# Linear attention and gated layers on one core: the attention denominators of four chunks in one PSUM tile, their reciprocals spread over the rows by DMA

## The chip, the cores and the metric

The kernel runs on one core of a Trainium2 chip. Its time is the device time of one execution in microseconds (us). TensorE (PE) multiplies, VectorE (DVE) and ScalarE (ACT) read its sums from PSUM and work on them, GpSimd (POOL) only fills constants, SyncE (SP) issues nearly all transfers.

## The reference

The input x has 2048 rows of 1024 numbers in bf16. Four layers follow each other: attention, gated, attention, gated. Each normalises its rows first and adds its result to x.

```python
# attention: 32 heads of 32
pq, pk = phi(q), phi(k)              # phi(t) = where(t > 0, t + 1, exp(t)) + 1e-6
kv  = einsum("bhsd,bhse->bhde", pk, v)
z   = einsum("bhsd->bhd", pk)        # per head: sum of pk over all rows
num = einsum("bhqd,bhde->bhqe", pq, kv)
den = einsum("bhqd,bhd->bhq", pq, z)[..., None] + 1e-6
x   = x + concat_heads(num / den) @ wo
# gated layer, F = 3584
x   = x + ((norm(x) @ w_gate) * (norm(x) @ w_up)) @ w_down
```

The change concerns `den`: one number for each head and row, by which the 32 elements of that head in `pq` are divided (the division is done on `pq`, ahead of the product with `kv`).

## The kernel before

Rows are taken in four groups g of 512. An attention layer has two parts. The first makes keys and values for all rows (`kv_chunk`, matmul at L230) and sums `pk` times `v` in three PSUM tiles (`kp`, L248), with a column of ones beside `v` that gives z. The second is a loop of steps i over the queries; nothing in it is reordered by a scheduler, each engine runs its instructions in the order in which the loop writes them.

In step i, `q_step` makes chunk c of group g (i = 8g + c): 128 of the 1024 query columns (four heads) for 512 rows, eight matmuls of 512 columns (L333). `phi` (L216 to L218) is an Exp on ACT and two operations on DVE; the last one frees the PSUM bank. Four steps later `den_step` multiplies the chunk by `zb[:, c, :]` (L341). `zb` is 128 by 128: z times a mask that is one inside each head's 32 by 32 block, so each denominator comes out in all 32 rows of its head. ACT makes the reciprocal as exp(-ln(d + 1e-6)) (L343, L344), and DVE writes `pq` times it into a tile `pqs` (L347). Twelve steps behind the query, `out_step` multiplies 128 rows of the scaled queries by M, eight matmuls (L354), and DVE adds the sum to X (L356).

M is `kv` times `wo`, folded once a layer: `finish_kv` masks the sums and writes `zb` (L298 to L302), `tr_kv` transposes at step 3, and `fold` (L318, two matmuls; one copy on ACT, L320, one on DVE, L322) runs at steps 4 to 11.

PSUM: query and output sums share a ring of four banks (`mm`), the sums of `kp`, denominators and folds a ring of three (`kv`). SBUF: weights, transposed inputs and M share a ring of 13 slots of 1 MB (`wp`); SP issues loads in program order and waits in that order for the slot of each. In the query loop it loads the first weights of the gated layer behind (wg, wu at L74; wd at L81): a pair at step 0, a pair and wd at step 14, wd at 17, 25, and three at 33; and it transposes the first normalised rows of the next layer (L171, steps 22 to 28). A ring `h` of four tiles of seven blocks (128 by 512) holds `pk`, `pqs` and the gated layer's products `hT`.

In the gated layer each of 28 steps f makes gate and up sums (L423, L427), ACT copies the gate (L430) into a tile `gs`, DVE multiplies (L433), and the down product follows (L459, L462).

Of the kernel before, what the change touches and what calls it, by code (L numbers as in the profile page):

```python
# [9 lines left out]
ALU = mybir.AluOpType  # L10
BF16 = mybir.dt.bfloat16
# [4 lines left out]
def kernel(  # L16
# [11 lines left out]
    nc = tc.nc  # L28
# [10 lines left out]
    FB = F // NB  # L39
    FPB = NB // P  # L40
    DC = D // NB
    HC = 7

    ctx.enter_context(tc.manual_schedule())

# [1 line left out]
    small = ctx.enter_context(tc.tile_pool(name="small", bufs=4))  # L47
    xnp = ctx.enter_context(tc.tile_pool(name="xnp", bufs=2))
    wp = ctx.enter_context(tc.tile_pool(name="wp", bufs=13))
    hp = ctx.enter_context(tc.tile_pool(name="hp", bufs=4))  # L50
    work = ctx.enter_context(tc.tile_pool(name="work", bufs=2))
    psum = ctx.enter_context(tc.tile_pool(name="psum", bufs=4, space=bass.MemoryType.PSUM))

    x_view = A_x[0].rearrange("(t p) d -> p t d", p=P)
# [62 lines left out]
    nc.gpsimd.memset(mask[:], 0.0)  # L117
    for b in range(4):
        nc.gpsimd.memset(mask[32 * b:32 * b + 32, 32 * b:32 * b + 32], 1.0)
    eps5 = const.tile([P, 1], F32, tag="eps5", name="eps5")  # L120
    nc.gpsimd.memset(eps5[:], 1e-5)
    eps6 = const.tile([P, 1], F32, tag="eps6", name="eps6")
# [91 lines left out]
    def phi(ps, dst):  # L214
        m = work.tile([P, NB], F32, tag="m", name="m", bufs=3)
        nc.scalar.activation(out=m[:], in_=ps[:], func=ACT.Exp)  # L216
        nc.vector.tensor_scalar(out=m[:], in0=m[:], scalar1=1.0, scalar2=1e-6, op0=ALU.min, op1=ALU.add)  # L217
        nc.vector.scalar_tensor_tensor(out=dst, in0=ps[:], scalar=0.0, in1=m[:], op0=ALU.max, op1=ALU.add)  # L218

    def layer_A(li, preload_B):  # L220
# [67 lines left out]

        kvm = work.tile([P, KD, P], BF16, tag="kvm", name="kvm", bufs=1)
        kvT = work.tile([P, KD, P], BF16, tag="kvT", name="kvT", bufs=1)  # L290
        zb = work.tile([P, KD, P], BF16, tag="zb", name="zb", bufs=1)
        z = work.tile([P, KD], F32, tag="z", name="z", bufs=1)

        def finish_kv():
            for b in range(3):
                nb = min(3, KD - 3 * b)
                src = kvp[b][:, 0:nb * VW].rearrange("p (c f) -> p c f", f=VW)
                nc.vector.tensor_copy(out=z[:, 3 * b:3 * b + nb], in_=src[:, :, P])  # L298
                for j in range(nb):
                    nc.vector.tensor_tensor(out=kvm[:, 3 * b + j, :], in0=src[:, j, 0:P], in1=mask[:], op=ALU.mult)  # L300
            for c in range(KD):
                nc.vector.tensor_scalar(out=zb[:, c, :], in0=mask[:], scalar1=z[:, c:c + 1], scalar2=None,  # L302
                                        op0=ALU.mult)

        def tr_kv():
# [15 lines left out]
                else:  # L321
                    nc.vector.tensor_copy(out=M[n][:, c, :], in_=ps[:])  # L322

        pq = {}
        pqs = {}

        def q_step(g, c):
            xnT = xnTs[(li, g)]
            w = wA["q"][c // (NB // P)]
            j = c % (NB // P)  # L330
            ps = mm_tile()
            for k in range(KD):
                nc.tensor.matmul(out=ps[:], lhsT=w[:, k, j * P:(j + 1) * P], rhs=xnT[:, k, :],  # L333
                                 start=(k == 0), stop=(k == KD - 1))
            pq[(g, c)] = work.tile([P, G], BF16, tag="pq", name="pq", bufs=6)
            phi(ps, pq[(g, c)][:])

        def den_step(g, c):
            p = pq.pop((g, c))
            dps = kv_tile("dps")  # L340
            nc.tensor.matmul(out=dps[:], lhsT=zb[:, c, :], rhs=p[:], start=True, stop=True)  # L341
            r = work.tile([P, G], F32, tag="r", name="r", bufs=2)
            nc.scalar.activation(out=r[:], in_=dps[:], func=ACT.Ln, bias=eps6[:], scale=1.0)  # L343
            nc.scalar.activation(out=r[:], in_=r[:], func=ACT.Exp, scale=-1.0)  # L344
            if c % 4 == 0:
                pqs[(g, c // 4)] = hp.tile([P, HC, G], BF16, tag="h", name="pqs")
            nc.vector.tensor_tensor(out=pqs[(g, c // 4)][:, c % 4, :], in0=p[:], in1=r[:], op=ALU.mult)  # L347

        def out_step(g, j):
            tl, n = divmod(j, DC)  # L350
            t = g * TPG + tl
            ps = mm_tile("ops")
            for c in range(KD):
                nc.tensor.matmul(out=ps[:], lhsT=pqs[(g, c // 4)][:, c % 4, tl * P:(tl + 1) * P],  # L354
                                 rhs=M[n][:, c, :], start=(c == 0), stop=(c == KD - 1))
            nc.vector.tensor_tensor(out=X[:, t, n * NB:(n + 1) * NB], in0=X[:, t, n * NB:(n + 1) * NB],  # L356
                                    in1=ps[:], op=ALU.add)

        LAG, OLAG = 4, 12
        NQ = NG * KD  # L360
        for i in range(NQ + OLAG):
            if i >= LAG and i - LAG < NQ:
                den_step(*divmod(i - LAG, KD))
            if i < NQ:
                q_step(*divmod(i, KD))
            if i == 0:
                for t in range(NT - TPG, NT):
                    kp(t)
                finish_kv()
                preload_B("p")  # L370
            if i == 3:
                tr_kv()
            if 4 <= i < 4 + KD:
                fold(i - 4)
            if i >= OLAG:
                out_step(*divmod(i - OLAG, KD))
            if i in (14, 17, 25, 33):
                preload_B({14: "pr", 17: "r", 25: "r", 33: "rrr"}[i])
            for u in range(TPG):
# [31 lines left out]
    def layer_B(li, stream):  # L411
        last = li == 3
        for g in range(NG):
            xnT = xnTs[(li, g)]
            hT = []
            nl, ng = (li, g + 1) if g + 1 < NG else (li + 1, 0)
            for f in range(KF):
                fb, j = divmod(f, FPB)
                if j == 0:
                    wg, wu = stream.have.pop((g, fb))  # L420
                gp = mm_tile("gp")
                for k in range(KD):
                    nc.tensor.matmul(out=gp[:], lhsT=wg[:, k, j * P:(j + 1) * P], rhs=xnT[:, k, :],  # L423
                                     start=(k == 0), stop=(k == KD - 1))
                up = mm_tile("up")
                for k in range(KD):
                    nc.tensor.matmul(out=up[:], lhsT=wu[:, k, j * P:(j + 1) * P], rhs=xnT[:, k, :],  # L427
                                     start=(k == 0), stop=(k == KD - 1))
                gs = work.tile([P, NB], F32, tag="gs", name="gs", bufs=2)
                nc.scalar.copy(out=gs[:], in_=gp[:])  # L430
                if f % HC == 0:
                    hT.append(hp.tile([P, HC, G], BF16, tag="h", name="hT"))
                nc.vector.tensor_tensor(out=hT[f // HC][:, f % HC, :], in0=gs[:], in1=up[:], op=ALU.mult)  # L433
                if j == FPB - 1:
                    stream.pair()
                    stream.rows()
                for u in range(TPG if nl < 4 else 0):
                    t = ng * TPG + u
                    if f == 6 + 4 * u:
                        ln_stats(nl, (t,))  # L440
                    if f == 7 + 4 * u:
                        ln_norm(nl, t)
                    if f == 8 + 4 * u:
                        tr_tile(nl, t)
            xnTs.pop((li, g))
            if g == NG - 1 and not last:
                wA["k"] = load_A(1)
                wA["v"] = load_A(2)
                wA["q"] = load_A(0)
                wA["o"] = load_wo()  # L450
            for tl in range(TPG):
                t = g * TPG + tl
                cuts = [(n * NB, (n + 1) * NB) for n in range(DC)]
                if last and t == NT - 1:
                    cuts[-1:] = [(D - NB, D - NB // 2), (D - NB // 2, D)]
                for lo, hi in cuts:
                    ps = kv_tile("dn", hi - lo)
                    for f in range(KF):
                        nc.tensor.matmul(out=ps[:], lhsT=hT[f // HC][:, f % HC, tl * P:(tl + 1) * P],  # L459
                                         rhs=stream.wd[f // 4][:, f % 4, lo:hi],  # L460
                                         start=(f == 0), stop=(f == KF - 1))
                    nc.vector.tensor_tensor(out=X[:, t, lo:hi], in0=X[:, t, lo:hi], in1=ps[:], op=ALU.add)  # L462
                    if last:
                        nc.sync.dma_start(out=o_view[:, t, lo:hi], in_=X[:, t, lo:hi])
# [47 lines left out]
```

## Time and profile before

| | |
|---|---|
| median of the runs | 1654.07 us (1654.0 to 1654.95, three runs) |
| the profiled execution's own time | 1654.75 us |
| its span, first to last instruction | 1652.9 us |
| granted TensorE clock | 1.00 |
| denominator matmuls (L341) | 64, each 379 ns long in the records |
| Ln and Exp of the reciprocals (L343, L344) | 64 each, 692 and 629 ns |
| scaling of the queries on DVE (L347) | 64, 685 ns |
| copies of M (L320 ACT, L322 DVE) | 16 each, 579 and 680 ns |
| query loop of the first attention layer | about 126 to 250 us |
| load of 1 MB, issue to landing (wg, wd) | 5.2 and 5.6 us, median |

A matmul's record is longer than the time for which it holds the array, since the next one starts before its end: the spacing of the starts tells its cost. In the rows of single instructions the first number is the start, the second the length, both in us from the start of the span; `L341` is a line of the kernel, `dps<-pq,zb` what is written from what. "Idle before" is what the engine waited for.

### The profile page before, as it was taken

What the parts mean: (1) busy time and instruction counts of PE and PEld (TensorE: products, weight loads), DVE (VectorE), ACT (ScalarE), POOL (GpSimd) and SP (SyncE); (2) the same over time, 40 slices, a digit from 0 to 9 for tenths busy, and PEclk for the clock granted to TensorE, in tenths of its full rate; (3) what the DMA queues carried; (4) which work ended last, traced back from release to release, by engine and by line L of the source; (5) the groups of instructions that cost most, each with busy time, mean ns of one, the idle gap of its engine ahead of it and who ended that gap; (6) DMA issues with size and microseconds to landing.
All of it is one profiled execution on the core that took longest, in us unless ns stands there. A gap on an engine that the chain in (4) does not pass through costs nothing.

```text
span 1652.9 us, 18521 instructions
## 1 busy us (share of the span) xinstructions
PE 1646.7 (100%) x7864; PEld 757.7 (46%) x7864; DVE 559.3 (34%) x985; ACT 368.0 (22%) x699; POOL 1.6 (0%) x17
## 2 busy tenths in 40 slices
PE   9999999999999999999999999999999999999999
PEld 4544444444444444444444544444444444444444
DVE  6537762311321231132155388522113212211111
ACT  4336541200210120021033375311002101100110
POOL 0000000000000000000000000000000000000000
PEclk9999999999999999999999999999999999999999
DMA  7433134631461263055132321346225514622400
GB/s 229 127 77 102 38 90 134 172 127 39 139 163 41 83 172 128 31 141 167 46 100 39 87 79 45 124 134 172 76 87 147 162 33 131 173 82 90 153 29 23
DMA packets 211250, 174.21 MB, mean 105 GB/s; under 512 B 66528, under 2 KB 202080, under 8 KB 211168
## 3 DMA queue, kind: packets, MB, share of 16 engines
q1 hardware_dynamic: 210880, 172.64, 36.2%
q8 instruction: 61, 1.00, 0.2%
q10 hardware_dynamic: 288, 0.39, 0.1%
q14 instruction: 21, 0.17, 0.0%
HBM read 153.09 MB, written 4.19 MB: 95 GB/s over the span
## 4 chain that ended last, share of the span: by engine, by line
PE 99%; DMA 0%; SPq 0%; ACT 0%; issue 0%; DVE 0%
PE dn L459 23%; PE up L427 23%; PE gp L423 23%; PE ps L230 13%; PE ops L354 7%; PE ps L333 7%; PE kvp L248 1%; PE dps L341 1%; PE mps L318 0%; DMA wv<-in_A_wqkv_dram 0%; SPq L97 0%; PE pt L180 0%; PE pt L308 0%; ACT xnT L182 0%; SPq L65 0%
## 5 line engine op out<-in xcount | busy, mean ns | idle before, releaser
L423 PE MATMUL gp<-xnT,wg 128*128 128x512 bf16 x1792 | 423.3, 379 | 0.0
L427 PE MATMUL up<-xnT,wu 128*128 128x512 bf16 x1792 | 423.3, 379 | 0.0
L459 PE MATMUL dn<-wd,hT 128*128 128x512 bf16 (+1 forms) x1820 | 388.1, 376 | 0.0
L433 DVE TENSOR_TENSOR hT<-gs,up 128x512 bf16<-128x512 f32 x224 | 154.0, 688 | 567.0 <-PE up L427 567.0
L430 ACT COPY gs<-gp 128x512 f32<-128x512 f32 x224 | 131.4, 586 | 945.8 <-PE gp L423 945.8
L459 PEld LDWEIGHTS <-hT 128*128 128x128 bf16 x1820 | 178.1, 98 | 209.0
L423 PEld LDWEIGHTS <-wg 128*128 128x128 bf16 x1792 | 175.4, 98 | 211.4
L427 PEld LDWEIGHTS <-wu 128*128 128x128 bf16 x1792 | 175.3, 98 | 211.4
L462 DVE TENSOR_TENSOR X<-X,dn 128x512 bf16<-128x512 bf16 (+1 forms) x65 | 44.1, 679 | 341.9 <-PE dn L459 341.9
L230 PEld LDWEIGHTS <-xnT 128*128 128x128 bf16 x1024 | 99.7, 98 | 120.2 <-ACT xnT L182 1.1
L333 PE MATMUL ps<-xnT,wq 128*128 128x512 bf16 x512 | 120.3, 379 | 0.0
L354 PE MATMUL ops<-M,pqs 128*128 128x512 bf16 x512 | 118.3, 379 | 0.0
L230 PE MATMUL ps<-wv,xnT 128*128 128x512 bf16 x512 | 112.8, 379 | 1.4 <-DMA wv<-in_A_wqkv_dram 0.8
L230 PE MATMUL ps<-wk,xnT 128*128 128x512 bf16 x512 | 112.6, 379 | 0.0
L216 ACT ACTIVATE m<-ps 128x512 f32<-128x512 f32 x128 | 76.4, 597 | 158.3 <-PE ps L230 130.4
L217 DVE TENSOR_SCALAR m<-m 128x512 f32<-128x512 f32 x128 | 54.1, 422 | 82.6 <-ACT m L216 81.8
L354 PEld LDWEIGHTS <-pqs 128*128 128x128 bf16 x512 | 50.1, 98 | 60.4
L333 PEld LDWEIGHTS <-wq 128*128 128x128 bf16 x512 | 50.0, 98 | 60.1 <-issue 0.6
L146 DVE BATCH_NORM_STATS2 st<-X 128x6 f32<-128x512 bf16 x120 | 76.7, 681 | 0.0
L343 ACT ACTIVATE r<-dps,eps 128x512 f32<-128x512 f32 x64 | 44.3, 692 | 54.1 <-PE dps L341 54.1
L347 DVE TENSOR_TENSOR pqs<-pq,r 128x512 bf16<-128x512 bf16 x64 | 43.8, 685 | 31.4 <-ACT r L344 31.4
L241 ACT CAST vb<-ps 128x512 bf16<-128x512 f32 x64 | 37.6, 588 | 62.1 <-PE ps L230 62.1
(45 smaller groups left out, 384.3 us busy)
## 6 DMA issues: line engine op xcount, KB each, us to landing
wg<-in_B_w_gate_dram SPq DMA_DIRECT2D x56, 1024.0 KB, 5.2
wu<-in_B_w_up_dram SPq DMA_DIRECT2D x56, 1024.0 KB, 6.9
wd<-in_B_w_down_dram SPq DMA_DIRECT2D x14, 1024.0 KB, 5.6
wk<-in_A_wqkv_dram SPq DMA_DIRECT2D x4, 1024.0 KB, 7.7
wq<-in_A_wqkv_dram SPq DMA_DIRECT2D x4, 1024.0 KB, 7.3
wo<-in_A_wo_dram SPq DMA_DIRECT2D x4, 1024.0 KB, 7.6
out_dram<-X SPq DMA_DIRECT2D x31, 128.0 KB, 1.7
X<-in_A_x_dram SPq DMA_DIRECT2D x14, 256.0 KB, 8.5
```

What stands on the lines that cost most here:

```text
L146: nc.vector.bn_stats(out=st[:, c, :], in_=X[:, t, c * FMAX:(c + 1) * FMAX])
L216: nc.scalar.activation(out=m[:], in_=ps[:], func=ACT.Exp)
L217: nc.vector.tensor_scalar(out=m[:], in0=m[:], scalar1=1.0, scalar2=1e-6, op0=ALU.min, op1=ALU.add)
L230: nc.tensor.matmul(out=ps[:], lhsT=xnT[:, k, tl * P:(tl + 1) * P], rhs=w[:, k, :], start=(k == 0), stop=(k == KD - 1))
L333: nc.tensor.matmul(out=ps[:], lhsT=w[:, k, j * P:(j + 1) * P], rhs=xnT[:, k, :], start=(k == 0), stop=(k == KD - 1))
L343: nc.scalar.activation(out=r[:], in_=dps[:], func=ACT.Ln, bias=eps6[:], scale=1.0)
L354: nc.tensor.matmul(out=ps[:], lhsT=pqs[(g, c // 4)][:, c % 4, tl * P:(tl + 1) * P], rhs=M[n][:, c, :], start=(c == 0), stop=(c == KD - 1))
L423: nc.tensor.matmul(out=gp[:], lhsT=wg[:, k, j * P:(j + 1) * P], rhs=xnT[:, k, :], start=(k == 0), stop=(k == KD - 1))
L427: nc.tensor.matmul(out=up[:], lhsT=wu[:, k, j * P:(j + 1) * P], rhs=xnT[:, k, :], start=(k == 0), stop=(k == KD - 1))
L430: nc.scalar.copy(out=gs[:], in_=gp[:])
L433: nc.vector.tensor_tensor(out=hT[f // HC][:, f % HC, :], in0=gs[:], in1=up[:], op=ALU.mult)
L459: nc.tensor.matmul(out=ps[:], lhsT=hT[f // HC][:, f % HC, tl * P:(tl + 1) * P], rhs=stream.wd[f // 4][:, f % 4, lo:hi], start=(f == 0), st ...
```

## The change

`den_step` is split. Steps, by the new line numbers:

- `q_step` writes phi straight into a tile of the ring `h`, which is now seven tiles of four chunks (`HC = 4`), in place of a tile of its own. The gated layer's `hT` uses tiles of four as well.
- `zb` is 128 by 32, by a mask `hmask` that has one eight columns wide strip for each head. `den_quad(u)` (steps 5, 9, ... 33) multiplies chunks 4u to 4u+3, each into 32 rows of one PSUM tile, with the matmul placed in a column quarter of the array (L353). One Ln and one Exp (L356, L357) then serve four chunks, and a DMA issued by ACT (L359) writes the 16 different rows, 32 KB, to a buffer in DRAM.
- `spread(u)`, behind the query of the same step, has ACT issue four transfers (L366). Each reads the four chunks' rows of one head, 8 KB, and writes them to 32 rows of `rb`: 256 KB each, 1 MB for a quad. `rb` has one buffer.
- `scale` (L372) multiplies the queries in place by `rb`, chunks 0 and 1 of a quad at step 4u+8, chunks 2 and 3 at step 4u+9.
- Output steps (L379, L381) run 16 steps behind the query instead of 12, and the eight folds (L324; copies L326 on ACT and L328 on DVE) stand at steps 4, 6, 7, 8, 10, 11, 12 and 14.
- `gs` takes its buffers from the ring `m` of three, which phi uses.

```diff
-    HC = 7
+    HC = 4
+    HW = 32
...
-    hp = ctx.enter_context(tc.tile_pool(name="hp", bufs=4))
+    hp = ctx.enter_context(tc.tile_pool(name="hp", bufs=7))
...
+    dramp = ctx.enter_context(tc.tile_pool(name="dramp", bufs=4, space=bass.MemoryType.DRAM))
...
+    hmask = const.tile([P, HW], F32, tag="hmask", name="hmask")
+    nc.gpsimd.memset(hmask[:], 0.0)
+    for b in range(4):
+        nc.gpsimd.memset(hmask[32 * b:32 * b + 32, 8 * b:8 * b + 8], 1.0)
...
-        zb = work.tile([P, KD, P], BF16, tag="zb", name="zb", bufs=1)
+        zb = work.tile([P, KD, HW], BF16, tag="zb", name="zb", bufs=1)
...
-            pq[(g, c)] = work.tile([P, G], BF16, tag="pq", name="pq", bufs=6)
-            phi(ps, pq[(g, c)][:])
-
-        def den_step(g, c):
-            p = pq.pop((g, c))
+            phi(ps, pq_at(i))
+
+        def den_quad(u):
             dps = kv_tile("dps")
-            nc.tensor.matmul(out=dps[:], lhsT=zb[:, c, :], rhs=p[:], start=True, stop=True)
-            r = work.tile([P, G], F32, tag="r", name="r", bufs=2)
+            for j in range(4):
+                i = 4 * u + j
+                nc.tensor.matmul(out=dps[HW * j:HW * j + HW, :], lhsT=zb[:, i % KD, :], rhs=pq_at(i),
+                                 start=True, stop=True, tile_position=(0, HW * j))
+            r = work.tile([P, G], F32, tag="r", name="r", bufs=1)
             nc.scalar.activation(out=r[:], in_=dps[:], func=ACT.Ln, bias=eps6[:], scale=1.0)
             nc.scalar.activation(out=r[:], in_=r[:], func=ACT.Exp, scale=-1.0)
-            if c % 4 == 0:
-                pqs[(g, c // 4)] = hp.tile([P, HC, G], BF16, tag="h", name="pqs")
-            nc.vector.tensor_tensor(out=pqs[(g, c // 4)][:, c % 4, :], in0=p[:], in1=r[:], op=ALU.mult)
+            rd = dramp.tile([4, 4, G], F32, tag="rd", name="rd")
+            nc.scalar.dma_start(out=rd[:].rearrange("h j n -> j h n"), in_=r[0:P:8, :])
+            rbs[u] = rd
+
+        def spread(u):
+            rd = rbs[u]
+            rb = work.tile([P, 4, G], F32, tag="rb", name="rb", bufs=1)
+            for h in range(4):
+                nc.scalar.dma_start(out=rb[HW * h:HW * h + HW, :, :].rearrange("p j n -> p (j n)"),
+                                    in_=rd[h, :, :].rearrange("j n -> (j n)").partition_broadcast(HW))
+            rbs[u] = rb
+
+        def scale(i):
+            nc.vector.tensor_tensor(out=pq_at(i), in0=pq_at(i), in1=rbs[i // 4][:, i % 4, :], op=ALU.mult)
...
-        LAG, OLAG = 4, 12
+        OLAG = 16
+        FOLD = [4, 6, 7, 8, 10, 11, 12, 14]
         NQ = NG * KD
         for i in range(NQ + OLAG):
-            if i >= LAG and i - LAG < NQ:
-                den_step(*divmod(i - LAG, KD))
+            if i % 4 == 1 and 8 <= i < NQ + 8:
+                for j in (2, 3):
+                    scale(i - 9 + j)
+            if i % 4 == 1 and 5 <= i < NQ + 5:
+                den_quad(i // 4 - 1)
             if i < NQ:
-                q_step(*divmod(i, KD))
+                q_step(i)
+            if i % 4 == 1 and 5 <= i < NQ + 5:
+                spread(i // 4 - 1)
+            if i % 4 == 0 and 8 <= i < NQ + 8:
+                for j in (0, 1):
+                    scale(i - 8 + j)
...
-            if 4 <= i < 4 + KD:
-                fold(i - 4)
+            if i in FOLD:
+                fold(FOLD.index(i))
...
-                gs = work.tile([P, NB], F32, tag="gs", name="gs", bufs=2)
+                gs = work.tile([P, NB], F32, tag="m", name="gs", bufs=3)
```

More of the change, by code (lines that the diff above doesn't have):

```diff
@@ L301, in finish_kv @@
             for c in range(KD):
-                nc.vector.tensor_scalar(out=zb[:, c, :], in0=mask[:], scalar1=z[:, c:c + 1], scalar2=None,
+                nc.vector.tensor_scalar(out=zb[:, c, :], in0=hmask[:], scalar1=z[:, c:c + 1], scalar2=None,
                                         op0=ALU.mult)
@@ L322, in fold, with pq_at, q_step @@
                     nc.vector.tensor_copy(out=M[n][:, c, :], in_=ps[:])
-        pq = {}
         pqs = {}
-        def q_step(g, c):
+        rbs = {}
+        def pq_at(i):
+            if i // HC not in pqs:
+                pqs[i // HC] = hp.tile([P, HC, G], BF16, tag="h", name="pq")
+            return pqs[i // HC][:, i % HC, :]
+        def q_step(i):
+            g, c = divmod(i, KD)
             xnT = xnTs[(li, g)]
@@ L334, in q_step @@
                                  start=(k == 0), stop=(k == KD - 1))
-            pq[(g, c)] = work.tile([P, G], BF16, tag="pq", name="pq", bufs=6)
-            phi(ps, pq[(g, c)][:])
-        def den_step(g, c):
-            p = pq.pop((g, c))
+            phi(ps, pq_at(i))
+        def den_quad(u):
             dps = kv_tile("dps")
-            nc.tensor.matmul(out=dps[:], lhsT=zb[:, c, :], rhs=p[:], start=True, stop=True)
-            r = work.tile([P, G], F32, tag="r", name="r", bufs=2)
+            for j in range(4):
[3 more added lines that the diff above has]
+            r = work.tile([P, G], F32, tag="r", name="r", bufs=1)
             nc.scalar.activation(out=r[:], in_=dps[:], func=ACT.Ln, bias=eps6[:], scale=1.0)
             nc.scalar.activation(out=r[:], in_=r[:], func=ACT.Exp, scale=-1.0)
-            if c % 4 == 0:
-                pqs[(g, c // 4)] = hp.tile([P, HC, G], BF16, tag="h", name="pqs")
-            nc.vector.tensor_tensor(out=pqs[(g, c // 4)][:, c % 4, :], in0=p[:], in1=r[:], op=ALU.mult)
+            rd = dramp.tile([4, 4, G], F32, tag="rd", name="rd")
[8 more added lines that the diff above has]
+            rbs[u] = rb
+            rbs[u] = rb
+        def scale(i):
+            nc.vector.tensor_tensor(out=pq_at(i), in0=pq_at(i), in1=rbs[i // 4][:, i % 4, :], op=ALU.mult)
         def out_step(g, j):
@@ L353, in out_step @@
             for c in range(KD):
-                nc.tensor.matmul(out=ps[:], lhsT=pqs[(g, c // 4)][:, c % 4, tl * P:(tl + 1) * P],
+                nc.tensor.matmul(out=ps[:], lhsT=pq_at(g * KD + c)[:, tl * P:(tl + 1) * P],
                                  rhs=M[n][:, c, :], start=(c == 0), stop=(c == KD - 1))
```

## The prediction

> **What bounds the kernel now.** I read the busy shares first, then the chain that ended last, then the stretches around the step that changes, then single instructions there.
>
> The page's busy shares and the chain by engine and line:
>
> ```profile
> PE 1646.7 (100%) x7864; PEld 757.7 (46%) x7864; DVE 559.3 (34%) x985; ACT 368.0 (22%) x699; POOL 1.6 (0%) x17
> ...
> PE 99%; DMA 0%; SPq 0%; ACT 0%; issue 0%; DVE 0%
> PE dn L459 23%; PE up L427 23%; PE gp L423 23%; PE ps L230 13%; PE ops L354 7%; PE ps L333 7%; PE kvp L248 1%; PE dps L341 1%; PE mps L318 0%; DMA wv<-in_A_wqkv_dram 0%; SPq L97 0%; PE pt L180 0%; PE pt L308 0%; ACT xnT L182 0%; SPq L65 0%
> ```
>
> TensorE is the chain, from end to end. The denominators (dps, L341) are 1% of it, so what this change can take away is small, and what it can add as a wait is paid in full. The stretches of the first attention layer (its start, its query steps without output steps, two mixed ones, its output steps alone); the columns are PE, weight loads, DVE and ACT busy, clock, DMA share and GB/s:
>
> ```profile
> 126.00:142.00 16.00, 15.97 (x104) 8.41 (x103) 11.44 (x34) 8.95 (x16) 0.00 (x0) 1.00 0.21 67
> 142.00:157.00 15.00, 15.00 (x71) 6.83 (x70) 14.79 (x27) 14.36 (x26) 0.00 (x0) 1.00 0.27 84
> 157.00:195.00 38.00, 38.00 (x178) 17.22 (x177) 27.32 (x47) 20.03 (x33) 0.00 (x0) 1.00 0.16 56
> 195.00:234.00 39.00, 39.00 (x183) 17.67 (x182) 30.59 (x55) 22.34 (x39) 0.00 (x0) 1.00 0.45 127
> 234.00:250.00 16.00, 16.00 (x76) 7.24 (x75) 7.29 (x12) 1.32 (x2) 0.00 (x0) 1.00 0.06 17
> ```
>
> The second line matters: where queries run without output steps, DVE is busy 14.79 of 15.00 us. The average of 34% hides that; a wait put into DVE's queue there can't be caught up. One step of that stretch, instruction by instruction (start, length):
>
> ```profile
> 147.65 0.38 PE L341 MATMUL dps<-pq,zb 128*128 128x512 bf16 x1
> 147.65 1.61 PEld L333 LDWEIGHTS <-wq 128*128 128x128 bf16 x8
> 147.86 1.89 PE L333 MATMUL ps<-xnT,wq 128*128 128x512 bf16 x8
> ...
> 148.37 0.70 ACT L343 ACTIVATE r<-dps,eps 128x512 f32<-128x512 f32 x1
> ...
> 149.11 0.63 ACT L344 ACTIVATE r<-r 128x512 f32<-128x512 f32 x1
> 149.11 0.68 DVE L322 CAST M<-mps 128x512 bf16<-128x512 f32 x1
> 149.37 0.31 PEld L318 LDWEIGHTS <-kvT 128*128 128x128 bf16 x2
> 149.59 0.59 PE L318 MATMUL mps<-wo,kvT 128*128 128x512 bf16 x2
> 149.77 0.69 DVE L347 TENSOR_TENSOR pqs<-pq,r 128x512 bf16<-128x512 bf16 x1
> ...
> 150.02 0.38 PE L341 MATMUL dps<-pq,zb 128*128 128x512 bf16 x1
> ```
>
> From one denominator matmul to the next are 2.37 us: eight query matmuls 1.73, two fold matmuls 0.43, the denominator 0.21. So a 512-column matmul holds the array for 0.216 us, though its record is 0.379 long; the 0.163 between them is pipeline that the next one overlaps.
>
> **Part by part.**
>
> *Removed from TensorE:* 64 denominator matmuls (32 a layer) of 0.216: 13.8 us, all on the chain.
>
> *Added to TensorE:* 16 quads of four 32-column matmuls. No row shows one. Least: all four stream at once, 0.216, so 3.5 us in all and 10.3 saved. Most: one after another, 0.864, with an emptied pipeline on entering and leaving (0.163 each) and a bare weight load (0.098): 1.29 each, 20.6, so 6.8 lost. I take one stream plus the two emptied pipelines and one load, 0.216+0.326+0.098 = 0.64: 16 of them are 10.2, **saving 3.6 us**. The reason for the middle: four column quarters hold separate weights, so nothing in the work forbids streaming together, but the matmuls before and after use the whole width. The Trainium skill, TensorEngine Tiling (Array Packing), Key Properties, states both halves: tiles operate independently, and a change of tiling mode drains the array. TensorE: Matmul & The Clock Gate, Part 3, gives 2.38x for three column tiles; with free switching the quads would be an estimated 3.5 to 4.5 us in all and the sum about 1655. No row here shows a switch.
>
> *ACT:* loses 48 Ln and 48 Exp (0.692 and 0.629: 63 us), gains 80 DMA issues. The two issues on its queue at the start last 0.39 and 0.45, so 31 to 36 us. In busy time a gain, but ACT isn't the bound; what counts is a new wait. Each spread (L366) stands in ACT's queue behind the query's Exp and waits until the 32 KB of reciprocals (L359) lie in DRAM. Let T be PE's arrival at quad u (step 4u+5). Sums are readable at T+0.6, Ln and Exp take 1.37 (148.37 to 149.74), the store is issued at T+1.95; the nearest small stores, of X to the output, land after 1.6 us, so T+3.55. Four issues hold ACT until T+5.2. The Exp of query 4u+6, ready at T+4.25, is queued behind it, then the fold's copy of M, which frees a bank of the ring of three for the next fold, and then DVE's half of phi. So 0.95 us of delay per quad. DVE's work in four such steps, by starts, is 4x(0.46+0.60) phi + 4x0.60 scale + 3x0.60 M = 8.4; PE's is 4x1.73+3x0.43+0.64 = 8.9. Some 0.4 to 0.5 is caught up; 0.5 stays for each of quads 0 to 2, and the fold's bank adds as much once: **2 us a layer** (0 if the phi lag is always covered, 3.5 if each quad pays its 0.95 and the bank).
>
> *The transfers:* 1 MB a quad in four parts of 256 KB. Near end: a 1 MB weight load lands in 5.2 us and the engines move 334 GB/s (158 to 162 us). Far end: the 256 KB load on ACT's queue took 3.4 us; four in series are 13.6. Nothing in the trace writes 32 rows alone; I take 7, nearer to the first, since four parts overlap their starts. They land at T+3.55+7 = T+10.5. DVE asks for them (L372) at step 4u+8, after that step's phi: T+0.64+4x1.73+2x0.43+1.8 = T+10.2. So quads 0 and 1 just hold. The Trainium skill, SBUF — State Buffer, Door 1, speaks against this form: 32 partitions reach 8 of 16 ports, 189 GB/s where 128 get 328. By it 1 MB needs an estimated 5.5 us of moving plus start and receipt, which is also about 7.
>
> Quad 2 is worse: the last fold now stands at step 14, not 11, and frees the two wo slots on which SP's first two wd loads wait (before, both were issued at 154.75). 2 MB so start beside spread 2, whose share halves: 3.2 us more. It lands at T+13.7 and is asked for at T+9.8. Behind the waiting scale in DVE's queue stand phi and the X additions, which free the four mm banks; they cover about three us. **1 us a layer** (0 to 4). Quads 3 to 6 lie among output steps, 3.45 us a step, and have some 4 us to spare: nothing, unless the spread takes over 11 us. Quad 7 (step 33) meets three wd loads and faster steps: the last group's output steps begin at T+0.64+7x1.73 = T+12.7 and need scale 31, which ends between T+13 and T+16: **1.5 us a layer** (0 to 4). With 0.5 for quads 0 and 1, waits are 5 a layer, **10 in all** (2 to 23).
>
> *Hidden or neutral, together:* narrower zb writes take DVE time off the layer's start. Output steps begin at 16, not 12: PE's work is the same, and the statistics of the next layer (steps 20 to 28) still follow their X tile (steps 17 to 23). wd is later by some 5 us and first read at 346.6; the transposes behind it on SP start at 192.87, long after. gs in m's ring and h tiles of four: ACT is idle 945.8 us ahead of the 224 gs copies and DVE 567.0 ahead of its products, which hides them; were that gone, each copy would cost 0.6. The extra POOL memsets (0.1 to 0.2 each) end before the first vb use.
>
> *Sum,* against the profiled execution's 1654.75 (span 1652.9 and 1.85 around it; 0.7 above the median): -3.6 +10 = +6.4, **1661**.
>
> **Rivals.** The cover holds (the other side): phi's lag and the spreads fit under PE's queue, ACT's Ln/Exp saving pays for its wait. For it: four mm banks, and ACT is lighter by 28 us; against: 14.79 of 15.00. Waits fall to nothing, 1654.75-3.6 = 1651 at my quad, 1644.5 at the least one; it decides once the waits are below what the quads save, by 3.3 us for a measurable gain.
> The change doesn't do what it says: the four don't stream together. Then the quads cost 20.6, +6.8; part of it gives the waits time, so these count 8: 1669.
> The spread is the bound: at over 11 us each, mixed quads wait too; each us beyond costs up to one us for each of 16 quads. At 12.5: 1661+16 = 1677 or so. For it: one 8 KB source read 32 times; against: DMA share of 0.16 to 0.45 in the mixed stretches.
> The parts cancel: waits of 3 to 4 us, 1654.
>
> **How the numbers follow.** Forecast 0.38, cover holds 0.27, no streaming together 0.14, spread the bound 0.10, cancelling 0.11. A measurement of this kernel tells some 0.2% (3.3 us) from no change: slower 0.38+0.14+0.10 = 0.62, same 0.11, faster 0.27. The range goes from the middle of the cover case, 1646, past no streaming, to the lower half of the spread case, 1675; the forecast alone is 1656 to 1667.
>
> **What would show it.** Quads: starts of the four L353 matmuls far less than 216 ns apart (right) or 216 (wrong); 0.5 to 0.8 us from the last matmul ahead of a quad to the first behind it. Waits: L366 on ACT waiting for the DMA of rd by about a microsecond a quad; L372 waiting for rb at quads 2 and 7; PE idle ahead of L324, L353 and L379, some 5 us a layer, in a chain that has ACT, DVE and DMA in it. The forecast is wrong if PE stays at 99% of the chain, or if L372 waits at every quad.

## The result and the profile after

The changed kernel takes 1671.16 us (median of four runs, 1670.38 to 1672.7) against 1654.03 for the kernel before: 17.1 us more, a ratio of 1.0105 [1.009, 1.012]. The profiled execution took 1670.72, its span is 1668.7.

The page of the changed kernel: busy shares, the chain by engine and by line, and two groups (the last columns are busy time, mean ns of one, idle time before them and what ended most of it):

```profile
PE 1637.5 (98%) x7709; PEld 753.0 (45%) x7864; DVE 552.3 (33%) x985; ACT 306.1 (18%) x603; POOL 2.1 (0%) x22
...
PE 92%; DMA 4%; DVE 2%; issue 1%; ACTq 1%; ACT 0%; DVEq 0%
PE up L461 23%; PE dn L493 23%; PE gp L457 23%; PE ps L236 13%; PE ops L379 5%; PE ps L345 4%; DMA rb<-rd 3%; DVE pq L372 1%; PE kvp L254 1%; DMA rd<-r 1%; ACTq L366 1%; DMA X<-in_A_x_dram 0%; DVE M L328 0%; DVE m L223 0%; DVE pq L224 0%
...
L379 PE MATMUL ops<-M,pq 128*128 128x512 bf16 x504 | 120.2, 389 | 12.0 <-DVE X L381 11.4
...
L372 DVE TENSOR_TENSOR pq<-pq,rb 128x512 bf16<-128x512 bf16 x64 | 41.0, 681 | 28.3 <-DMA rb<-rd 25.9
```

TensorE was 99% of the chain and is 92%. What came in is the new path: the store of the reciprocals (rd), the spread (rb), its issue on ACT (L366) and the scaling behind it (L372). DVE waits 25.9 us for spreads over both layers, and TensorE waits 11.4 us in its output steps for DVE's additions (L381), which stand behind the scaling in DVE's queue.

The denominators themselves became cheap. A quad where nothing waits, in the order of time of the changed kernel (start, length):

```profile
183.98 0.40 PE L353 MATMUL dps<-pq,zb 128*32 128x512 bf16 x4
184.31 1.90 PE L345 MATMUL ps<-xnT,wq 128*128 128x512 bf16 x8
```

Four matmuls lie inside 0.40 us, hardly longer than the record of one, and the next query matmul starts 0.33 us after the first of them. Sixteen quads hold the array for 5.3 us, where 64 matmuls of 0.216 held it for 13.8.

Quad 0 of the first attention layer, ACT and TensorE:

```profile
138.57 1.10 ACTq L359 DMA_DIRECT2D rd<-r  x1
...
140.70 1.77 ACTq L366 DMA_DIRECT2D rb<-rd  x4
...
142.57 0.60 ACT L222 ACTIVATE m<-ps 128x512 f32<-128x512 f32 x1 [2.20 <-issue]
...
143.06 0.58 ACT L326 CAST M<-mps 128x512 bf16<-128x512 f32 x1
...
143.69 0.38 PE L324 MATMUL mps<-wo,kvT 128*128 128x512 bf16 x1 [0.82 <-ACT M L326]
```

ACT stands at the spread until the store is in DRAM, issues for 1.77 us, then does the Exp of the next query and only then the copy of M, for whose bank TensorE waits. This is the wait that was foreseen.

Quad 2, all engines:

```profile
160.81 1.96 SPq L83 DMA_DIRECT2D wd<-in_B_w_down_dram  x2
160.95 2.88 ACTq L366 DMA_DIRECT2D rb<-rd  x4
...
172.77 1.29 DVE L372 TENSOR_TENSOR pq<-pq,rb 128x512 bf16<-128x512 bf16 x2 [4.40 <-DMA rb<-rd]
...
174.72 1.89 PE L379 MATMUL ops<-M,pq 128*128 128x512 bf16 x8 [1.69 <-DVE X L381]
...
175.90 1.73 ACTq L366 DMA_DIRECT2D rb<-rd  x4
...
177.67 0.60 ACT L222 ACTIVATE m<-ps 128x512 f32<-128x512 f32 x1 [7.29 <-DVE X L381]
```

Two loads of wd (1 MB each) are issued at the same moment. The four issues on ACT last 2.88 us in place of 1.73, and the spread lands 11.8 us after its first issue instead of 7. Then comes a wait that nobody had named: `rb` has one buffer, so the spread of quad 3 can't be issued before the last scaling of quad 2 has read it. ACT stands at that issue until 175.90 and delays the Exp of a query by 7.29 us.

Quad 7, all engines, and the chain of the same stretch (start, length):

```profile
213.38 9.20 SPq L83 DMA_DIRECT2D wd<-in_B_w_down_dram  x3
...
225.00 0.40 PE L353 MATMUL dps<-pq,zb 128*32 128x512 bf16 x4
...
226.85 0.52 ACTq L359 DMA_DIRECT2D rd<-r  x1
233.05 1.73 ACTq L366 DMA_DIRECT2D rb<-rd  x4
...
240.01 1.29 DVE L372 TENSOR_TENSOR pq<-pq,rb 128x512 bf16<-128x512 bf16 x2 [8.60 <-DMA rb<-rd]
...
241.96 16.34 PE L379 MATMUL ops<-M,pq 128*128 128x512 bf16 x62 [4.36 <-DVE X L381]
```

```profile
226.85 5.96 DMA rd<-r
...
234.34 5.65 DMA rb<-rd
...
241.96 7.28 PE ops L379 x21
```

The store of 32 KB takes 6.0 us; ahead of it on the engines are loads of wd whose last issue ends at 222.6 (from 226 to 230 us the engines still move 386 to 391 GB/s). The spread that follows is as fast as any, 6.95 us from its first issue. TensorE has run out of work by then. And the 21 matmuls behind its pause take 7.28 us, where 21 times 0.216 and one pipeline of 0.163 are 4.7. The stretches of the changed kernel say why (PE, weight loads, DVE, ACT, POOL busy, clock, DMA share, GB/s):

```profile
237.00:242.00 5.00, 0.64 (x4) 0.24 (x3) 1.99 (x4) 0.00 (x0) 0.00 (x0) 0.84 0.34 69
242.00:244.00 2.00, 2.00 (x5) 0.65 (x5) 2.00 (x4) 0.00 (x0) 0.00 (x0) 0.50 0.00 0
244.00:246.00 2.00, 2.00 (x6) 0.74 (x5) 1.34 (x3) 0.00 (x0) 0.00 (x0) 0.50 0.00 0
246.00:248.00 2.00, 2.00 (x8) 0.74 (x7) 0.25 (x1) 0.00 (x0) 0.00 (x0) 0.70 0.00 0
```

After the pause TensorE works at half clock for some five microseconds.

### The profile page after: what moved, and what is told of

It is laid out like the page before. It is cut to its first block, busy times and chain, and to the rows that moved or that the text cites. A ratio compares the mean times of both kernels' runs of the same rounds, so it can differ in the third digit from the quotient of the medians.

```text
span 1668.7 us, 18381 instructions
## 1 busy us (share of the span) xinstructions
PE 1637.5 (98%) x7709; PEld 753.0 (45%) x7864; DVE 552.3 (33%) x985; ACT 306.1 (18%) x603; POOL 2.1 (0%) x22
## 4 chain that ended last, share of the span: by engine, by line
PE 92%; DMA 4%; DVE 2%; issue 1%; ACTq 1%; ACT 0%; DVEq 0%
PE up L461 23%; PE dn L493 23%; PE gp L457 23%; PE ps L236 13%; PE ops L379 5%; PE ps L345 4%; DMA rb<-rd 3%; DVE pq L372 1%; PE kvp L254 1%; DMA rd<-r 1%; ACTq L366 1%; DMA X<-in_A_x_dram 0%; DVE M L328 0%; DVE m L223 0%; DVE pq L224 0%
## 5 line engine op out<-in xcount | busy, mean ns | idle before, releaser
L379 PE MATMUL ops<-M,pq 128*128 128x512 bf16 x504 | 120.2, 389 | 12.0 <-DVE X L381 11.4
L379 PEld LDWEIGHTS <-pq 128*128 128x128 bf16 x512 | 50.9, 100 | 75.7 <-issue 17.6
L372 DVE TENSOR_TENSOR pq<-pq,rb 128x512 bf16<-128x512 bf16 x64 | 41.0, 681 | 28.3 <-DMA rb<-rd 25.9
L381 DVE TENSOR_TENSOR X<-X,ops 128x512 bf16<-128x512 bf16 x64 | 43.1, 680 | 17.3 <-PE ops L379 17.2
```

The lines of the kernel that those rows point to most:

```text
L372: nc.vector.tensor_tensor(out=pq_at(i), in0=pq_at(i), in1=rbs[i // 4][:, i % 4, :], op=ALU.mult)
L379: nc.tensor.matmul(out=ps[:], lhsT=pq_at(g * KD + c)[:, tl * P:(tl + 1) * P], rhs=M[n][:, c, :], start=(c == 0), stop=(c == KD - 1))
```

## The experiments

Two theories went into the first runs. One (A, where the expectations use letters): the spreads of quads 2 and 7 come late because loads of weights lie beside them on the DMA engines, and TensorE waits for that. The rival (B): the transfers hold ACT, and the one buffer `rb` hands the delay of one quad to the next. Each text below says what its theories expect of its run. The times of the kernel before in the three series were 1654.06, 1653.75 and 1654.09. As a second measure I use the distance on TensorE from one quad's first matmul to the next one's in the first attention layer (for quad 7, to the first gate matmul).

**e1: no transfers.**

```diff
-            nc.scalar.dma_start(out=rd[:].rearrange("h j n -> j h n"), in_=r[0:P:8, :])
...
-        def spread(u):
...
-            nc.vector.tensor_tensor(out=pq_at(i), in0=pq_at(i), in1=rbs[i // 4][:, i % 4, :], op=ALU.mult)
+            nc.vector.tensor_tensor(out=pq_at(i), in0=pq_at(i), in1=rone[:, i % 4, :], op=ALU.mult)
```

> Leaves out the store of the reciprocals and the four transfers of each quad; the scaling multiplies by a constant tile of ones, so the division by the denominators is missing from the result. Everything else is the changed kernel: quads, ring of four-chunk tiles, lags, fold steps, loads. Theory A (the loss is waiting for the transfers; the quads themselves hold the array 0.33 us each, as the trace of the changed kernel shows from 183.98 to 184.31): 1654.0 - 13.8 + 5.3 = 1645.5, within 1644 to 1648. Rival C (the switch of the array's columns, the longer lag or the tile ring cost as well): 1652 or more.

Measured: 1646.95, ratio 0.9958 [0.9943, 0.9973]. That is as theory A expected: the rest of the change, quads, lags, rings and fold steps, gains 7.1 us. The store and the spread cost 24.2. By quads, in us:

| | 0 to 1 | 1 to 2 | 2 to 3 | 3 to 4 | 7 to gate |
|---|---|---|---|---|---|
| changed kernel | 10.12 | 9.95 | 9.50 | 17.87 | 33.35 |
| e1 | 8.63 | 8.90 | 9.50 | 14.25 | 26.24 |
| difference | 1.49 | 1.05 | 0 | 3.62 | 7.11 |

The others are equal to 0.01. The second attention layer shows 1.34, 1.38, 0, 2.26 and 5.61. Both layers together make 23.9 of the 24.2, so this table is the whole loss, and the delay of quad 2 is paid behind quad 3.

**e2: two buffers for `rb`** (kvT moves into another tile's place to make room; its users follow).

```diff
-            rb = work.tile([P, 4, G], F32, tag="rb", name="rb", bufs=1)
+            rb = work.tile([P, 4, G], F32, tag="rb", name="rb", bufs=2)
```

> Two buffers for rb; the room comes from kvT taking over kvm's buffer. Theory A (transfers land late because weight loads run beside them, at quads 2 and 7): the spread of quad 3 no longer waits for the scaling of quad 2, which frees ACT some 4 us earlier once a layer, but quads 2 and 7 land as late as before: 1667 to 1671. Rival B (ACT's queue, held for 7.3 us by the one buffer of rb, is the main loss): 1655 to 1662.

Measured: 1661.36, ratio 1.0049 [1.0033, 1.0065], so 9.8 us of the loss go. That lies in the range of rival B (1655 to 1662). But not for B's reason: from quad 3 to 4, where ACT stood at the one buffer, only 0.84 is gained (17.03); most comes behind quad 7 (29.01, 4.3 less), where the single instruction and the stretches show:

```profile
239.84 10.38 PE L380 MATMUL ops<-M,pq 128*128 128x512 bf16 x46 [2.54 <-DVE X L382]
```

```profile
237.00:242.00 5.00, 2.46 (x12) 0.99 (x11) 4.11 (x7) 0.00 (x0) 0.00 (x0) 1.00 0.00 0
242.00:246.00 4.00, 3.95 (x20) 1.81 (x19) 2.75 (x5) 0.00 (x0) 0.00 (x0) 1.00 0.00 0
```

The pause is 1.8 us shorter, and after it the clock is 1.00. The buffer's part in the loss is real, but a good part of its gain is that of the clock. The four runs of e2 spread from 1659.45 to 1665.97; in the slowest the mean clock is 0.998, so there a half clock seems to have come back.

**e3: loads of wd ordered at later steps.**

```diff
-            if i in (14, 17, 25, 33):
-                preload_B({14: "pr", 17: "r", 25: "r", 33: "rrr"}[i])
+            if i in (14, 18, 25, 38):
+                preload_B({14: "p", 18: "rr", 25: "r", 38: "rrr"}[i])
```

> The loads of w_down move: from steps 14, 17, 25, 33 (one, one, one, three) to 18, 25, 38 (two, one, three), away from the spreads of quads 2 and 7. Theory A: the waits for rb at quads 2 and 7 go, and with them the idle PE ahead of the output steps (6.0 us a layer) and the half clock behind the longer of these (about 2.7): 17 to 20 us less, 1651 to 1654. Rival B (ACT's queue): less than 5 us, 1666 or more.

Measured: 1668.55, ratio 1.009 [1.0075, 1.0105]. By its time alone that is B's (1666 or more) and a blow to A, but the issues on SP's queue are where they were:

```profile
161.13 1.88 SPq L83 DMA_DIRECT2D wd<-in_B_w_down_dram  x2
...
212.46 9.64 SPq L83 DMA_DIRECT2D wd<-in_B_w_down_dram  x3
```

The changed kernel has them at 160.81 and 213.38, and the one between at 197.99 (here 197.52). SP runs ahead of the steps and waits for nothing but the slots, so a later line in the loop moves no load. The run therefore says nothing on A.

**e6: the same loads on ACT's queue, behind the spreads**, where a program order does hold them back.

```diff
-    def load_rows(i):
+    def load_rows(i, q=None):
...
-        nc.sync.dma_start(out=v, in_=wd_v[:, i * 4:(i + 1) * 4, :])
+        (q or nc.sync).dma_start(out=v, in_=wd_v[:, i * 4:(i + 1) * 4, :])
...
-                preload_B({14: "pr", 17: "r", 25: "r", 33: "rrr"}[i])
+                preload_B({14: "p", 18: "rr", 25: "r", 34: "rrr"}[i])
...
-                    self.rows()
+                    self.rows(nc.scalar)
```

> The changed kernel, with the six early w_down loads of each layer issued from ACT's queue, behind the spreads of quads 3, 5 and 7 (steps 18, 25, 34), so that they can't run beside the store and the spreads of quads 2 and 7. Theory A (these loads make them late): from quad 3 to quad 4 the 3.6 us, and behind quad 7 most of the 7.1 us, go in each layer: 1652 to 1657. Theory B (one buffer of rb, ACT's wait for the store): 1663 or more.

Measured: 1654.81, ratio 1.0006 [0.9997, 1.0015]. With only the queue and the time of these six loads changed, 16.4 of the 24.2 us are gone, as A expected: quad 3 to 4 takes 15.29 and the stretch behind quad 7 26.70, against 14.25 and 26.24 without transfers. Of TensorE's waits in the first layer that are left, the longest and the shortest (us in total, times, longest):

```profile
PE mps L324 <- ACT M L326: 1.9, 2, 1.1
...
PE ops L379 <- DVE X L381: 0.2, 1, 0.2
```

The wait for X additions has fallen from 6.0 us to 0.2; what stays is the hold of ACT at the early quads. At quad 7 the single instructions on ACT show the store:

```profile
224.86 0.52 ACTq L359 DMA_DIRECT2D rd<-r  x1
227.01 1.73 ACTq L366 DMA_DIRECT2D rb<-rd  x4
```

The spread follows the store's issue by 2.15 us, where it took 6.2 in the changed kernel: with the loads of wd behind it, the store is as quick as at quad 0 (138.57 to 140.70). The spread, 6.86 us to its first reader, is no quicker. The spread of quad 2, without the loads beside it, is read 7.2 us after its first issue instead of 11.8. So A is right for quads 2 and 7; at quads 0 and 1, where the loss is as before (10.11 and 10.38), ACT is held as B says.

**e7: half the bytes.** Chunks 2 and 3 of each quad are scaled by the reciprocals of chunks 0 and 1.

```diff
-            rb = work.tile([P, 4, G], F32, tag="rb", name="rb", bufs=1)
+            rb = work.tile([P, 2, G], F32, tag="rb", name="rb", bufs=1)
...
-                                    in_=rd[h, :, :].rearrange("j n -> (j n)").partition_broadcast(HW))
+                                    in_=rd[h, 0:2, :].rearrange("j n -> (j n)").partition_broadcast(HW))
```

> Each of the four transfers carries two chunks of reciprocals instead of four, 128 KB, 512 KB a quad; the other two chunks are scaled by the reciprocals of the first two, so the result is not the attention's. Count of transfers, store, queue and lags stay. If the landing time is bytes: it comes some 3 us earlier, the loss at quads 2 and 7 falls to a third: 1655 to 1660. If it is fixed cost (issues of 0.43 us, start and receipt): less than 1.5 us earlier, 1665 or more.

Measured: 1653.52, ratio 1.0 [0.999, 1.0009], better than expected. The store, all 80 issues and the one buffer are still there, and quads 2 and 7 cost almost nothing (15.00 and 26.25). Quad 7's store still takes 4.0 us, but the half spread 4.2 instead of 7.0: most of the landing time is bytes. Quads 0 and 1 cost what they did (10.09, 9.95): that wait does not depend on the bytes.

**e4: store and spread on GpSimd's queue.**

```diff
-            nc.scalar.dma_start(out=rd[:].rearrange("h j n -> j h n"), in_=r[0:P:8, :])
+            nc.gpsimd.dma_start(out=rd[:].rearrange("h j n -> j h n"), in_=r[0:P:8, :])
...
-                nc.scalar.dma_start(out=rb[HW * h:HW * h + HW, :, :].rearrange("p j n -> p (j n)"),
+                nc.gpsimd.dma_start(out=rb[HW * h:HW * h + HW, :, :].rearrange("p j n -> p (j n)"),
```

> The store and the four transfers are issued by POOL, which has nothing else to do, so ACT never waits for a transfer; sizes and places stay. Rival B: ACT's waits go (2.1 to 2.5 us for the store at each quad of the query steps, 7.3 at quad 3) and with them the idle PE ahead of the folds and quads: 9 us or more, 1662 or less. Theory A: DVE still waits for rb at quads 2 and 7, so more than half of the loss stays: 1662 to 1668.

Measured: 1686.17, ratio 1.0203 [1.0175, 1.0231]; both theories missed. Quad 0 to 1 is 8.63, as without transfers, so ACT was the holder there. But DVE now waits for `rb` six times in the first layer, 28.7 us in all. Quad 0:

```profile
141.90 1.94 POOL L366 DMA_DIRECT2D rb<-rd  x4 [1.73 <-DMA rd<-r]
...
152.72 1.29 DVE L372 TENSOR_TENSOR pq<-pq,rb 128x512 bf16<-128x512 bf16 x2 [5.47 <-DMA rb<-rd]
```

Quad 0's spread lands at 152.6, over 9 us after its last issue. On ACT's queue it was read 5.6 us after that, though both kernels issue a load of wu (1 MB) at this moment. It is not the queue alone: at quads 1 and 7 the spread takes as long from first issue to reading as on ACT's queue (6.96 and 7.07 us, against 7.08 and 6.97); at quads 0, 2, 5 and 6, beside loads or transposes of SP, it takes 9.0 to 12.6. How the two queues share the engines, no run here tells.

**e10: store and spread on SP's queue** (as e4, with `nc.sync`).

> The changed kernel with the store and the four transfers issued by SP instead of ACT. SP works in program order, so the weight loads behind a spread start after it, and ACT neither waits for the store nor spends 1.7 us a quad on issues. Theory: both of the shown causes (loads beside quads 2 and 7, ACT's queue held) shrink, but the pair of gate and up loads, issued ahead of quad 0 until now, moves behind quad 2 and puts 4 MB ahead of quad 3: 1650 to 1657. If what remained in the run with the loads behind the spreads (1654.8) was not ACT's queue: 1655 or more.

Measured: 1657.00, ratio 1.0019 [1.001, 1.0028]. That is the upper end of what was expected. ACT is free (8.63 from quad 0 to 1), but from quad 1 to 2 it takes 10.85, more than in the changed kernel (9.95): DVE now waits 0.92 us for the spread of quad 0, and TensorE stands twice for 0.95 ahead of a fold. So of the 2.54 us that quads 0 and 1 cost in the first layer, freeing ACT alone gives back 0.6; by these waits the spread is then the holder. Since SP issues in order, loads of weights wait behind the spreads. But the store and the spread of quad 3 also wait behind loads:

```profile
163.86 0.43 SPq L76 DMA_DIRECT2D wg<-in_B_w_gate_dram  x1
164.34 0.66 SPq L76 DMA_DIRECT2D wu<-in_B_w_up_dram  x1
165.04 3.09 SPq L83 DMA_DIRECT2D wd<-in_B_w_down_dram  x1
...
177.40 1.74 SPq L366 DMA_DIRECT2D rb<-rd  x4
...
184.44 1.29 DVE L372 TENSOR_TENSOR pq<-pq,rb 128x512 bf16<-128x512 bf16 x2 [4.15 <-DMA rb<-rd]
```

From quad 4 to 5 it takes 16.92, 2.7 more than without transfers.

**e13: e10 with the pair of wg and wu ordered at step 10** in place of 14.

```diff
-            if i in (14, 17, 25, 33):
-                preload_B({14: "pr", 17: "r", 25: "r", 33: "rrr"}[i])
+            if i in (10, 14, 17, 25, 33):
+                preload_B({10: "p", 14: "r", 17: "r", 25: "r", 33: "rrr"}[i])
```

> As the run with SP's queue, and the pair of gate and up loads written at step 10 instead of 14, so that it runs behind the spread of quad 1 and not ahead of quad 3. The idle PE ahead of folds and quads 0 to 2 goes (2.3 us a layer), quads 2 and 7 land in time or within 1 us: 1648 to 1652.

Measured: 1656.04, ratio 1.0012 [1.0003, 1.0021], a miss. The pair now lies ahead of quad 2's store, and the scaling there waits 4.88 us: 2.0 us are lost from quad 3 to 4 (16.25) instead of 2.7 from 4 to 5, and 1 to 2 takes 10.85 as in e10. The scaling of quad 7 waits 4.53, but so it does in e6 (4.46), and TensorE hardly feels it (26.76 to the gate matmul). Moving one load in front of one spread only chooses which quad pays.

**e5: time for the spread, on ACT's queue.** Two buffers as in e2, the spread issued a step later, the scaling four steps later, output steps at 18, loads as in e3 with the last three at step 40.

```diff
-        OLAG = 16
+        OLAG = 18
...
-            if i % 4 == 1 and 8 <= i < NQ + 8:
+            if i % 4 == 1 and 12 <= i < NQ + 12:
...
-            if i % 4 == 1 and 5 <= i < NQ + 5:
+            if i % 4 == 2 and 6 <= i < NQ + 6:
                 spread(i // 4 - 1)
```

> Everything later by the steps that the transfers need: spread one step after the store (4u+6), scaling at 4u+12 and 4u+13, two buffers of rb, output steps 18 behind the query. Sizes, issuing queue and number of transfers stay. If the whole loss is waiting in the order of the queues (theory A and B together), what is left is the kernel without transfers: 1647 to 1650, faster than before. If the transfers cost something that no lag hides (their bytes beside the weight loads, the issues on ACT), 1653 or more.

Measured: 1654.83, ratio 1.0007 [0.9997, 1.0017], five above what the first theory gave and in the range of the second (1653 or more). ACT's queue again:

```profile
160.62 3.44 ACTq L367 DMA_DIRECT2D rb<-rd  x4
160.69 2.46 SPq L83 DMA_DIRECT2D wd<-in_B_w_down_dram  x2
...
164.11 0.59 ACT L327 CAST M<-mps 128x512 bf16<-128x512 f32 x1 [3.03 <-DMA rb<-rd]
...
166.43 0.38 PE L354 MATMUL dps<-pq,zb 128*32 128x512 bf16 x1 [1.77 <-DVE pq L224]
```

ACT no longer waits for the store, but at quad 2 its four issues last 3.44 us where they mostly last 1.7, and behind them the copy of M and the query's Exp are late by that. It is the smaller part: 1.7 us from quad 3 to 4, in the first layer alone. The issues of 1.7 us at quads 0 and 1 cost 2.4 us in the first layer and 2.1 in the second (9.99 and 9.69, then 9.69 twice, against 8.64 four times in the next run, e11). The rest is behind quad 7.

**e11: e13 with the same time given** (two buffers, scaling four steps later, output steps at 18).

> As the run before, with two buffers of rb, scaling at 4u+12 and 4u+13 and output steps 18 behind the query. Nothing waits for a transfer any more: the time of the kernel without transfers, 1647 to 1649, 0.3 to 0.4% faster than the kernel before. If it stays above 1651, the transfers cost something apart from their place in the queues.

Measured: **1647.47**, ratio 0.9961 [0.9948, 0.9973]. It is faster than both kernels, by 6.6 us than the one before, and equal within half a microsecond to the kernel without transfers. Its page, the chain:

```profile
PE 98%; DVE 1%; DMA 0%; ACT 0%; issue 0%; ACTq 0%; DVEq 0%
```

The trace shows no wait of TensorE in its first query loop. No engine that TensorE needs stands at an issue, and a spread may land several microseconds late without holding anything. Which of its changes (two buffers, later scaling, later output steps) matters most was not separated; e13 and e5 show that the queue alone and the time alone both leave some 8 us.

**e9: TensorE kept busy at quad 7.** The changed kernel with 16 matmuls that feed nothing, ahead of output step 40.

```diff
+            if i == NQ + 8:
+                fps = kv_tile("fps")
+                for _ in range(16):
+                    nc.tensor.matmul(out=fps[:], lhsT=warm[:, 0:P], rhs=warm[:], start=True, stop=True)
```

> The changed kernel with 16 more matmuls of 512 columns (3.5 us of work whose sums nobody reads) ahead of output step 40, where PE stood idle for 4.4 and 3.8 us. If the half clock that the trace shows after that wait (0.50 from 242 to 246 us) comes from the idle time and costs its 2 to 3 us a layer, the kernel with more work is faster: 1665 to 1668. If it does not depend on the idle time: 1671, or up to 1674 where the filler is added to the path.

Measured: 1667.37, ratio 1.0081 [1.0066, 1.0096]. That is as expected if the half clock comes from the idle time: 3.8 us faster than the changed kernel, with 3.5 us of matmuls more in each layer. Single instructions and a stretch:

```profile
238.24 3.62 PE L412 MATMUL fps<-warm 128*128 128x512 bf16 x16
243.04 14.05 PE L379 MATMUL ops<-M,pq 128*128 128x512 bf16 x62 [1.18 <-DVE X L381]
```

```profile
242.00:244.00 2.00, 0.96 (x5) 0.48 (x5) 2.00 (x4) 0.00 (x0) 0.00 (x0) 1.00 0.00 0
```

The data come no earlier: TensorE resumes 1.1 us later than in the changed kernel, where the same 62 matmuls took 16.34. The 2.3 us between are the price of the half clock in the first layer, measured by itself.

## Why the prediction was wrong in size

The direction and the places were right: TensorE leaves 99% of the chain, DVE waits for `rb` at quads 2 and 7 and nowhere else for long, and the path goes through ACT, DMA and DVE. Of the forecast of 1661, +6.4 against the profiled execution, the medians show +17.1. By its own steps, both layers together (waits from the table of e1 and its line for the second layer):

| step | predicted | measured |
|---|---|---|
| quads for 64 matmuls | -3.6 | -7.1 (e1) |
| quads 0 and 1, ACT held by the store (predicted with quad 2's hold) | +5 | +5.3 |
| quad 2 beside two loads of wd | +2 | +5.9 |
| quad 7 | +3 | +12.7 |
| sum | +6.4 | +16.8 |

*The quads.* I took 0.64 us for one; it is 0.33. One stream of 0.216 was right. The two emptied pipelines and the bare weight load were too much: entering and leaving cost 0.11 together. The Trainium skill, TensorEngine Tiling (Array Packing), Key Properties, says that a change of tiling mode drains the array; if there is a drain, it is inside those 0.11. By starts alone 8.5 us are saved, 1.4 more than e1's median shows; where the rest goes was not looked for.

*Quads 0 and 1.* The hold of ACT and its path (store, issue, Exp, copy of M) were as predicted; e4 and e10, which take the transfers off ACT, both have 8.63 from quad 0 to 1. That the sum fits is partly luck: of the 5, 1 is the hold at quad 2 and 1 a wait of DVE at quads 0 and 1, which the first layer puts at 0 and 0.21 us; the 3 that are left for the hold itself became 5.3. And the hold hides a second one: with ACT free the spread is late there (e10, e13).

*The spread alone* was taken at 7 us: quad 1's is first issued at 150.75 and read at 157.8, and the engines move 202 to 208 GB/s in its middle. That is far below the 334 that I had as one end, and somewhat above the 189 that the Trainium skill, SBUF — State Buffer, Door 1, gives for 32 rows.

*Quad 2 failed in two terms.* Its landing was put at T+13.7, T being 156.6, and came at T+16.1 (T+14.8 in the second layer). I had the shared bandwidth, but the store took 2.5 us and not 1.6, and the four issues on ACT 2.88 and not 1.7 (1.79 in the second layer). And I counted what stands in DVE's queue behind the wait, but not in ACT's, which waits for the same `rb` at the next spread. e2 puts the buffer's part at 0.84 us in the first layer, e6 that of the loads and all that follows from them at 2.6.

*Quad 7 failed most.* The step said that the spread lands at T+10.5 and that DVE's work is then late by up to T+16. It assumed 1.6 us for the store, measured on small stores that stood behind nothing. This one stands behind loads of wd and takes 6.0, so the data came at T+15.0 (second layer: the spread is issued 4.7 us after the store, and the data came at T+14.4). I had put the loads beside the spread and not beside the store, although the store's landing was a term of the sum. The output steps ran out of work at T+12.6 (I had T+12.7), so the pause was 4.4 us and not 1.5.

*The clock was no step at all.* The sum priced a pause of TensorE at its length and put nothing for what follows it. In the first layer 2.6 of the 7.1 us behind quad 7 are half clock after the pause, in the second some 1.8.

The rivals: that the cover holds fell; e1 and e11 show that its 1646 to 1651 was there to be had, but not with these transfers on this queue. That the four don't stream together fell. That the spread is the bound holds only where loads lie beside it or its store: quads 3 to 6 cost nothing.

## What to carry to other kernels

A change that trades a little work on the bound engine for a transfer on a path must be costed at the moment of each transfer: list every load that is in flight when it is issued, the small store ahead of it included, and ask for each buffer and each queue who stands still until it lands. Put such transfers on a queue whose engine computes nothing, and leave them several microseconds and a second buffer; here that, with one pair of loads ordered earlier, turned +17.1 us into -6.6. Either alone left some 8 us of it. Price a pause of TensorE of two microseconds and more as a range: its length, and up to some 2.6 us on top for a half clock, which came here with eight of thirteen such pauses.

## What the runs showed of the hardware

- After pauses of 4.36 and 3.79 us (changed kernel), 3.17 (e3) and 4.68 and 3.44 (e4, second layer) TensorE's granted clock was 0.50 for a while; after 2.54 (e2) and 1.18 us (e9) it stayed at 1.00. The length alone does not decide: it also stayed at 1.00 after 3.79 and 2.95 us in the first layer of e4 and after 2.98 in the second of e3, and it fell around pauses of 2.71 and 2.63 (e4) and of 1.97 us (e3, second layer). Each half clock lasted 3.4 or 6.8 us in the records, the part inside the pause counted in. The Trainium skill, TensorE: Matmul & The Clock Gate, HAM oscillation, puts the limit near 3.4 us; these runs don't bear out a limit at one length. What decides below and above it was not looked for.
- Sixteen matmuls a layer that feed nothing made the kernel 3.8 us faster.
- A store of 32 KB let the next transfer go 2.1 us after its issue with nothing ahead of it, and 6.2 us after it behind loads of 1 MB (4.7 in the second layer).
- Four issues on ACT's queue mostly lasted 1.7 us, but 2.88 and 3.44 at quad 2 beside issues of SP. SP's issues are not shown to be the cause: in e6 the four last 2.75 at the same quad, where SP issues nothing, and in the second layer of the changed kernel 1.79 beside two loads. In all ten cases of over 2.1 us on ACT's queue the DMA records have a packet of the kind `instruction` during the issues or within a microsecond before them; that this is the cause is not shown.
- With one buffer and the same lags the kernel took 1657.00 us with the transfers on SP's queue, 1671.16 on ACT's and 1686.17 on GpSimd's.

Two of the pauses that go against a limit at one length, as a single instruction and the stretch behind it, in e4 and then in e3:

```profile
247.62 1.67 PE L379 MATMUL ops<-M,pq 128*128 128x512 bf16 x7 [3.79 <-DVE X L381]
```

```profile
247.00:249.00 2.00, 1.38 (x7) 0.66 (x7) 2.00 (x4) 0.00 (x0) 0.00 (x0) 1.00 0.00 0
```

```profile
1001.46 2.56 PE L379 MATMUL ops<-M,pq 128*128 128x512 bf16 x8 [1.97 <-DVE X L381]
```

```profile
1002.60:1005.90 3.30, 3.30 (x9) 1.15 (x8) 2.46 (x6) 0.60 (x1) 0.00 (x0) 0.50 0.72 181
```
